# Routing filler, GpSimd subtractions tied to comparisons, and three 512-token tiles in a fused attention and two-MoE kernel

## The chip, the cores and the metric

The program runs on one core of one Trainium2 chip. The time is the device time of the program in microseconds, and each number for a kernel is the median of several runs. One further execution of the kernel was taken by the hardware profiler; all rows of the trace come from that one.

## The reference

```python
# attention: 4 batches, 8 heads, 576 positions, head size 64, causal window of 64
scores = q @ k.T / sqrt(64); softmax over the window; x = attn @ v     # 2304 tokens x 512
# dense layer
h = x @ w_in                                # 512 -> 2048
g = where(h > 0, h, exp(min(h, 0)) - 1)
x = g @ w_out                               # 2048 -> 512
# routed layer: 8 experts, 288 tokens each
logits = x @ w_gate
order = argsort(-logits.flatten())          # best token-expert pairs first
for idx in order:                           # greedy: a token takes the expert unless it is full
    tok, e = idx // 8, idx % 8
    if assigned[tok] >= 0 or counts[e] >= 288: continue
    assigned[tok] = e; counts[e] += 1
for e in range(8):
    out[mask_e] = relu(x[mask_e] @ w1[e]) @ w2[e]    # 512 -> 1024 -> 512
```

The assignment is a sequential greedy choice over 18432 pairs, so the logits must be very exact. The kernel therefore holds most operands as a pair of half-precision numbers, a high and a low part, and multiplies three of the four combinations.

## The kernel before

**Stages.** The tokens form 18 chunks of 128. Attention works chunk by chunk and writes its output, transposed, into tiles of tokens (`TILES`, line 360: five of 256 and two of 512). `layer1` (line 371) multiplies a tile by `w_in`, and ScalarE, GpSimd and VectorE make the activation and its two parts. `layer2` (line 447) multiplies by `w_out`, 48 matmuls of 512 columns for a chunk, and then leaves the chunk in three steps: ScalarE copies the sums out of PSUM, ScalarE rounds them to a high part, GpSimd subtracts to get the low part (line 469). A DMA writes both to `x2d` in DRAM (line 470). The last chunk alone uses VectorE for the low part (line 465). `gate` (line 412) computes the logits of a tile straight from the layer-1 result, with the matrix G2 that `prep_g2` (line 181) makes out of transposing DMAs into the one buffer `wt`; `x2_logits` does it for the first six chunks from `x2d`.

**Order.** `weave` (line 18) takes from several generators in proportion to declared totals, so the program order before line 950 is: `layer2` of tiles 0, 1, 2 and `layer1` of 3 and 4 between the attention chunks, then `layer1` of tiles 5 and 6. The framework's planner orders each engine's queue by priority and by its own estimate of times. From line 960 TensorE keeps the program order exactly (`pinned`).

**Routing** (line 546) needs all logits. It runs 7 phases; each finds a threshold in 5 digit steps and then does some bookkeeping. A digit step is a ring between two engines: VectorE makes the digit `D` (L612) and compares it with 32 values (L618); TensorE counts with 6 small matmuls (L621); VectorE reads the counts from PSUM (L625); 3 matmuls (L629); VectorE reads again (L631); 1 matmul (L635, or L638 in the last step). After the steps come L642 to L661, the matmuls L665 and L667, and L670 to L691, which give the value `M` for the next phase. In the phases from the fourth on, GpSimd does a part of that bookkeeping (L650 to L676 where `P_` stands, and L695 to L698 in all but the last). In the sixth phase GpSimd also makes two index tables (L701, L703). After the seventh phase VectorE builds the assignment (L706 to L716), TensorE sums it (L720, L721), VectorE makes positions and one-hot tables (L725 to L744), 18 matmuls (L748) turn them into row numbers, and L750 writes `idx`.

**Filler.** The small matmuls leave TensorE idle, so `fill` (line 950) lays the 576 matmuls of `layer2` for the last 12 chunks (1536 tokens) between them: each `yield W[n]` in the routing takes W[n] of them. The list `W` (line 948) gives 16 before and 8 inside the last gate, 33 before the phases, 69 in each phase (2 + 5 x 9 + 5 + 6 + 11), 4 and 3 at the two yields around L720, 6 and 4 around L748, and the 19 that remain follow when the routing is done. `dummies` (line 542) are matmuls whose results nobody reads, 8 at DM1 after L721 and 8 at DM2 after L748.

**Experts.** Each expert's weights come as four raw quarters of 1 MB into three buffers (`load_quarter`), and `split_expert` (line 773) turns each into high and low parts in 16 steps. During the filler experts 0 and 1 are split aside: ScalarE scales and rounds (L784, L785), GpSimd subtracts (L787), one step to every 17 filler matmuls. The other six are split by ScalarE and VectorE (L789, L790), two experts ahead of their use. `gather` (line 796) fetches the rows of an expert by `idx` from `x2d`; the first must wait for `idx` and for the last write to `x2d`.

Of the kernel before, what the change touches and what calls it, by code (L numbers as in the profile page):

```python
# [13 lines left out]
OP = mybir.AluOpType  # L14
# [25 lines left out]
def attention_moe_moe2_kernel(ctx: ExitStack, tc: tile.TileContext, q, k, v, w_in, w_out, w_gate, w1, w2, out):  # L40
# [316 lines left out]
    a2_ctx = ExitStack()  # L357

    NF32 = 2
    TILES = [256, 256, 256, 256, 256, 512, 512]  # L360
    T0 = [sum(TILES[:t]) for t in range(len(TILES))]


# [4 lines left out]
    def tile_n(t):  # L368
        return TILES[t]

# [73 lines left out]
            yield 300  # L444


    def layer2(t, chunks=None):
        fg = 1024 // tile_n(t)
        for i in range(tile_n(t) // 128) if chunks is None else chunks:
            c = T0[t] // 128 + i  # L450
            px = bank("mm", 3)
            m = 0
            for f in range(NF):
                g = GT[t][f // fg]
                for a, b in ((0, 0), (0, 1), (1, 0)):
                    pe(nc.tensor.matmul(px, g[:, f % fg, a, 128 * i:128 * i + 128], wo[f // 2][:, b, f % 2, :],  # L456
                                        start=m == 0, stop=m == 3 * NF - 1))
                    m += 1
                    yield 216
            xs = work.tile([128, 2, DM], F16, name="xs")  # L460
            x32 = work.tile([128, DM], F32, name="r", bufs=3)

            if c == NCH - 1:
                nc.scalar.activation(xs[:, 0], px, AF.Copy, scale=2.0 ** -11)
                nc.vector.scalar_tensor_tensor(xs[:, 1], px, 2.0 ** -11, xs[:, 0], op0=OP.mult, op1=OP.subtract)
            else:
                nc.scalar.activation(x32, px, AF.Copy, scale=2.0 ** -11)  # L467
                nc.scalar.activation(xs[:, 0], x32, AF.Copy)
                nc.gpsimd.tensor_tensor(xs[:, 1], x32, xs[:, 0], op=OP.subtract)
            nc.sync.dma_start(x2d[c * 128:(c + 1) * 128, :], xs.rearrange("p a d -> p (a d)"))  # L470

# [61 lines left out]
    def mid(ap, n):  # L535
        return ap[:, None, :].to_broadcast([ap.shape[0], n, ap.shape[1]])

    DM1 = 8
    DM2 = 8


# [4 lines left out]
    def routing():  # L546
# [50 lines left out]
        for ph in range(E - 1):  # L597
# [3 lines left out]
            for s in range(NS):  # L601
                ge = tl("ge", [128, NCH // 3, K, 3], BF, 2)
                if s == 0:
                    D, kk = M, r["k32"]
                else:

                    Mc = M
                    if s < NS - 1:
                        Mc = tl("Mc", [128, NCH], I32, 2)
                        V.tensor_scalar(Mc, M, -(K ** (NS - 1 - s)), None, op0=OP.bitwise_and)  # L610
                    D, kk = tl("D", [128, NCH], BF), r["k1" if s < NS - 1 else "k0"]
                    V.tensor_scalar(D, Mc, lo[:, 0:1], float(K) ** (s + 1 - NS), op0=OP.subtract, op1=OP.mult)  # L612
                pc = bank("sc", 2)
                for g0, g1 in ((0, SPL), (SPL, NCH // 3)):
                    if g0 == g1:
                        continue
                    d = D.rearrange("p (g i) -> p g i", i=3)[:, g0:g1, None, :].to_broadcast([128, g1 - g0, K, 3])
                    V.tensor_tensor(ge[:, g0:g1], d, kk[:, None].to_broadcast([128, g1 - g0, K, 3]), op=OP.is_ge)  # L618
                    yield W[3 if g0 == 0 else 4]
                    for g in range(g0, g1):  # L620
                        pe(T.matmul(pc[:3 * K, :3 * E], ge[:, g].rearrange("p k i -> p (k i)"),  # L621
                                    C[:, 3 * g:3 * g + 3].rearrange("p i e -> p (i e)"), start=g == 0,
                                    stop=g == NCH // 3 - 1))
                co = tl("co", [3 * K, 3 * E], F16)
                V.tensor_copy(co, pc[:3 * K, :3 * E])  # L625
                yield W[14]
                pk = bank("sc", 2)
                for i in range(3):
                    pe(T.matmul(pk[:K, :E], r["third"][:, i], co[:, i * E:(i + 1) * E], start=i == 0, stop=i == 2))  # L629
                full = tl("full", [K, E + 1], BF)  # L630
                V.tensor_scalar(full[:, :E], pk[:K, :E], float(CAP), 0.0, op0=OP.is_ge, op1=OP.max,  # L631
                                accum_out=full[:, E:])
                yield W[5]
                if s < NS - 1:
                    pe(T.matmul(lo[:, 0:1], r["wt"][:, s], full[:, E:], start=s == 0, stop=True, skip_group_check=True))  # L635
                else:
                    hi = bank("tp", 2)
                    pe(T.matmul(hi[:, :E + 1], r["ones"][:K], full, start=True, stop=True))  # L638
# [81 lines left out]
        pe(T.matmul(pr[:, :E], r["one"], r["ebase"][0:1], start=True, stop=False))  # L720
        pe(T.matmul(pr[:, :E], r["tri"], rk[:, :, NCH - 1], start=False, stop=True))  # L721
        yield W[16]
        dummies(DM1)
        t = tl("ts", [128, E, NCH])
        V.tensor_tensor(t, rk, bc(pr[:, :E], NCH), op=OP.add)  # L725
        V.tensor_tensor(t, t, AT_, op=OP.mult)
# [46 lines left out]
    def split_expert(e, aside=False):  # L773
        W1[e], W2[e] = [], []
        for i in range(4):
            st = RAW[e, i].rearrange("p (g n) -> p g n", n=512)
            for g in range(4):
# [4 lines left out]
                if aside:  # L782
                    with tc.issue_after(last["act"]):
                        nc.scalar.activation(st[:, g], st[:, g], AF.Copy, scale=64.0)  # L784
                        nc.scalar.activation(t[:, 0, c], st[:, g], AF.Copy)  # L785
                    with tc.issue_after(last["pool"]):
                        nc.gpsimd.tensor_tensor(t[:, 1, c], st[:, g], t[:, 0, c], op=OP.subtract)  # L787
                else:
                    dv(nc.scalar.activation(t[:, 0, c], st[:, g], AF.Copy, scale=64.0))  # L789
                    dv(nc.vector.scalar_tensor_tensor(t[:, 1, c], st[:, g], 64.0, t[:, 0, c], op0=OP.mult,  # L790
                                                      op1=OP.subtract))
                if g == 3:
                    load_quarter()
                yield 500

# [132 lines left out]
    def attend(a, b):  # L928
        return attention(range(a, b)), (b - a) * AT
# [4 lines left out]
          (chain(split_win(), *(prep_wout(j) for j in range(4))), 24), attend(A0, A1))  # L934
    w64_ctx.close()
    a2.append(a2_ctx.enter_context(tc.tile_pool(name="a2", bufs=2)))
    weave((layer2(0), UT), attend(A1, A1 + 2))
    weave((layer2(1), UT), attend(A1 + 2, A1 + 5))
    weave((chain(layer1(3), layer2(2)), 2 * UT), attend(A1 + 5, A1 + 9), (prep_g2(range(NF)), NF * 8 * 75))
    weave((chain(layer1(4), gate(3), gate(4)), UT * 1.25), attend(A1 + 9, NCH + 1), (x2_logits(range(6)), 18 * 100))  # L940
    a2_ctx.close()
    att_ctx.close()
    late = ExitStack()
    slabB = late.enter_context(tc.tile_pool(name="slabB", bufs=10))
    rpool = late.enter_context(tc.tile_pool(name="rpool", bufs=2))
    routing_consts(rpool)
    weave((chain(layer1(5, [slabB] * 8), gate(5), layer1(6, [slabB] * 2 + [slabA] * 6)), UT * 3))
    W = [1, 4, 2, 5, 0, 2, 5, 6, 11, 4, 16, 2, 6, 4, 2, 28, 3]

    def fill():  # L950
        for _ in range(3):
            load_quarter()
        p = chain(split_expert(0, True), split_expert(1, True))
        for i, _ in enumerate(chain(*(layer2(t) for t in range(3, 7)))):
            if i % 17 == 16 and i < 24 * 17:
                next(p, None)
            yield
        weave((p, 1))
# [2 lines left out]
    xs = fill()  # L961
    for _ in range(W[10]):
        next(xs, None)
    for _ in gate(6):
        for _ in range(W[11]):
            next(xs, None)
    rt_gen = routing()
# [5 lines left out]
            next(xs, None)  # L973
    for _ in xs:
        pass
    pinned.clear()
    late.close()
    moe = ctx.enter_context(tc.tile_pool(name="moe", bufs=2))
# [2 lines left out]
    for e in range(E):  # L981
# [3 lines left out]
        ss = [(expert(e, xe_first() if e == 0 else None, tail if e == E - 1 else None), 24000.0)]  # L985
        if e + 1 < E:
            gather(e + 1)
        sp = split_expert(e + 2) if e < E - 2 else iter(())
        ss.append((chain(take(sp, 8 if e < E - 2 else 0), xe_t(e + 1) if e < E - 1 else iter(()), sp), 9400.0))
        if e > 0:  # L990
            ss.append((o_rows(e - 1), 2000.0))
        weave(*ss)
# [31 lines left out]
```

## Time and profile before

| what | value |
|---|---|
| median of 3 runs | 821.84 us (820.53 to 821.99) |
| profiled execution | 817.73 us, its span 816.0 us |
| TensorE busy | 762.2 us (93%) |
| VectorE, ScalarE, GpSimd busy | 444.8, 368.6, 214.7 us |
| mean granted TensorE clock | 0.973 of full speed |

The span runs from the first to the last instruction. [...]

### The profile page before, as it was taken

Reading aid. Unit: us, or ns where it says so; the run is one execution under the profiler, and the core shown is the slowest. Engines: PE = TensorE matmul, PEld = TensorE weight load, DVE = VectorE, ACT = ScalarE, POOL = GpSimd, SP = SyncE. Lnnn points to the kernel's source line nnn. Section 1 sums busy time; section 2 is a strip of 40 time slices with the busy share of each in tenths; the row PEclk is TensorE's granted clock in tenths of the full one; section 3 lists DMA queues with packets and bytes.
Section 4 is the critical chain, followed back from the end, with each engine's and each line's share of the span. In section 5 each row is a group of like instructions: output and inputs, shape, how many; then the busy total and the mean of one; then the engine's idle time right before and its main releaser. Section 6 shows DMA issues by size and latency. Waiting matters only on the chain. (4 is left out here: it accounts for less than half of the span.)

```text
span 816.0 us, 16645 instructions
## 1 busy us (share of the span) xinstructions
PE 762.2 (93%) x6746; PEld 508.6 (62%) x6746; DVE 444.8 (55%) x1091; ACT 368.6 (45%) x895; POOL 214.7 (26%) x323
## 2 busy tenths in 40 slices
PE   7888899899998999999998999998759999999996
PEld 4666688645786587545453444443338888888886
DVE  4886599821465346554555565565806555546110
ACT  3556775714654446444466230100205665556222
POOL 3000002121031032644576342324532212221002
PEclk9999999799999999999999999999869999999999
DMA  9998134506365344001023230000329789997001
GB/s 241 300 266 213 25 99 169 104 24 133 86 139 104 77 92 104 2 1 52 1 91 129 78 117 27 14 27 14 103 88 209 238 245 273 198 248 196 20 21 50
DMA packets 122509, 94.23 MB, mean 115 GB/s; under 512 B 99200, under 2 KB 99200, under 8 KB 122432
## 3 DMA queue, kind: packets, MB, share of 16 engines
q1 hardware_dynamic: 119360, 83.72, 39.4%
q0 software_dynamic: 3072, 9.44, 4.3%
q8 instruction: 53, 0.87, 0.4%
q14 instruction: 24, 0.20, 0.1%
HBM read 69.22 MB, written 9.44 MB: 96 GB/s over the span
## 5 line engine op out<-in xcount | busy, mean ns | idle before, releaser
L456 PE MATMUL ps_mm<-slab,g 128*128 128x512 f16 x864 | 214.3, 382 | 0.0
L401 PE MATMUL ps_mm<-xt,slab 128*128 128x256 f16 (+1 forms) x960 | 154.7, 317 | 0.0
L401 PEld LDWEIGHTS <-slab 128*128 128x128 f16 x960 | 91.1, 98 | 49.0 <-issue 0.8
L456 PEld LDWEIGHTS <-g 128*128 128x128 f16 x864 | 74.6, 99 | 75.2 <-issue 7.2
L855 PE MATMUL ps_mm<-xet,slab 128*128 128x288 f16 (+1 forms) x840 | 101.6, 279 | 0.0
L406 POOL TENSOR_SCALAR r<-r 128x512 f32<-128x512 f32 x56 | 41.5, 742 | 198.2 <-ACT r L405 197.7
L889 PEld LDWEIGHTS <-slab 128*128 128x128 f16 x960 | 78.6, 98 | 16.2
L855 PEld LDWEIGHTS <-slab 128*128 128x128 f16 x840 | 77.7, 100 | 17.5
L790 DVE SCALAR_TENSOR_TENSOR slab<-raw,slab 128x512 f16<-128x512 f32 x96 | 62.5, 688 | 16.9 <-ACT slab L789 14.9
L861 DVE SCALAR_TENSOR_TENSOR h<-ps_mm,h 128x288 f16<-128x288 f32 x64 | 29.3, 457 | 76.7 <-ACT h L860 75.5
L889 PE MATMUL ps_sc<-h,slab 128*128 128x288 f16 (+1 forms) x480 | 70.1, 262 | 0.0
L889 PE MATMUL ps_tp<-h,slab 128*128 128x288 f16 (+1 forms) x480 | 69.8, 262 | 0.0
L404 ACT ACTIVATE r<-ps_mm 128x512 f32<-128x512 f32 x56 | 33.7, 605 | 74.8 <-PE ps_mm L401 51.6
L287 ACT ACTIVATE sm<-ps_sc,mx 128x128 f32<-128x128 f32 x144 | 50.8, 380 | 26.3 <-DVE mx L285 26.0
L389 PE MATMUL ps_mm<-xt,slab 128*128 128x256 f32 x256 | 61.1, 394 | 0.8 <-DVE slab L107 0.8
L409 DVE TENSOR_TENSOR g<-r,g 128x512 f16<-128x512 f32 x56 | 39.1, 704 | 38.2 <-POOL g L408 38.1
L467 ACT ACTIVATE r<-ps_mm 128x512 f32<-128x512 f32 x17 | 10.2, 600 | 103.8 <-PE ps_mm L456 103.7
L789 ACT ACTIVATE slab<-raw 128x512 f16<-128x512 f32 x96 | 55.3, 621 | 0.0
L389 PEld LDWEIGHTS ps_mm<-xt,slab 128*128 128x128 f32 x256 | 49.0, 196 | 9.3 <-issue 1.1
L407 DVE TENSOR_TENSOR r<-ps_mm,r 128x512 f32<-128x512 f32 x56 | 38.5, 690 | 29.3 <-POOL r L406 29.3
L830 POOL DMA_INDIRECT out_dram<-orow,idx x24 | 22.2, 924 | 114.4 <-ACT orow L844 112.7
L408 POOL TENSOR_SCALAR g<-r 128x512 f16<-128x512 f32 x56 | 35.7, 641 | 52.6 <-DVE r L407 32.8
(208 smaller groups left out, 1143.0 us busy)
## 6 DMA issues: line engine op xcount, KB each, us to landing
raw<-in_moe_w_dram SPq DMA_DIRECT2D x32, 1024.0 KB, 6.1
slab<-in_moe_w_in_dram SPq DMA_DIRECT2D x16, 512.0 KB, 7.4
st<-in_moe_w_out_dram SPq DMA_DIRECT2D x16, 512.0 KB, 3.9
x2d<-xs SPq DMA_DIRECT2D x18, 256.0 KB, 3.1
vp<-vn SPq DMA_DIRECT2D x35, 128.0 KB, 3.8
qn<-in_q_dram SPq DMA_DIRECT2D x16, 256.0 KB, 4.6
kn<-in_k_dram SPq DMA_DIRECT2D x16, 256.0 KB, 3.6
vn<-in_v_dram SPq DMA_DIRECT2D x16, 256.0 KB, 3.1
```

Of the source, the lines that this page charges most:

```text
L287: nc.scalar.activation(P[c, blk][:, i], SC[blk][:, i], AF.Exp, bias=mx[:, blk, i:i + 1], accum_out=rs[:, blk, i:i + 1])
L389: nc.tensor.matmul(ph[:, i], wi32[d, (f + i) // 8].bitcast(F32)[:, c], XT[t][:, d, :n], start=d == 0, stop=d == ND - 1)
L401: nc.tensor.matmul(ph[:, i], wi[d, (f + i) // 8][:, a, (f + i) % 8 * 128:((f + i) % 8 + 1) * 128], XT[t][:, b, d, :n], start=m == 0, stop= ...
L406: nc.gpsimd.tensor_scalar(r, r, -1.0, A_H, op0=OP.add, op1=OP.mult)
L407: nc.vector.tensor_tensor(r, ph, r, op=OP.max)
L408: last["pool"] = nc.gpsimd.tensor_scalar(hi, r, 1.0, 1.0, op0=OP.mult, op1=OP.mult).ins
L409: nc.vector.tensor_tensor(lo, r, hi, op=OP.subtract)
L456: pe(nc.tensor.matmul(px, g[:, f % fg, a, 128 * i:128 * i + 128], wo[f // 2][:, b, f % 2, :], start=m == 0, stop=m == 3 * NF - 1))
L789: dv(nc.scalar.activation(t[:, 0, c], st[:, g], AF.Copy, scale=64.0))
L790: dv(nc.vector.scalar_tensor_tensor(t[:, 1, c], st[:, g], 64.0, t[:, 0, c], op0=OP.mult, op1=OP.subtract))
L855: nc.tensor.matmul(ph[:, r], W1[e][d][:, a, f * 128:(f + 1) * 128], XET[e][:, b, d, r], start=m == 0, stop=m == 3 * ND - 1)
L889: nc.tensor.matmul(po[:, :n], w[:, a, f % 2, d * 128:(d + 1) * 128], H2[e][:, b, f, r], start=m == 0, stop=m == 3 * NF2 - 1)
```

## The change

The token tiles become three of 256 and three of 512, and the stages before the routing are dealt out anew. During the filler, the GpSimd subtractions, those of `layer2` and those of the aside split, are put on a list `later`. In each digit step, after the first comparison is issued, one is taken off the list with a dependency on that comparison; what must follow it (the DMA to `x2d`, the load of the next quarter) is issued with it. Only expert 0 is split aside, one step to every 24 filler matmuls; expert e + 1 is split within expert e. The dummies at DM1 go. `W` takes 73 filler matmuls in each phase (3 + 5 x 9 + 6 + 6 + 13), 4 and 4 around L720, and none around L748: 576 in all by then.

```diff
-    TILES = [256, 256, 256, 256, 256, 512, 512]
+    TILES = [256, 256, 256, 512, 512, 512]
...
+    later = []
+    def low_parts(behind=None):
+        lo, v, hi, then = later.pop(0)
+        ins = nc.gpsimd.tensor_tensor(lo, v, hi, op=OP.subtract)
+        if behind is not None:
+            tc.add_manual_dep(ins.ins, behind.ins.name, mybir.DependencyInfo(
+                mybir.DependencyClass.Sync, mybir.DependencyReason.SCHED_ONLY), reason="beside PSUM reads")
+        if then is not None:
+            then()
...                                                            # layer2
-                nc.gpsimd.tensor_tensor(xs[:, 1], x32, xs[:, 0], op=OP.subtract)
-            nc.sync.dma_start(x2d[c * 128:(c + 1) * 128, :], xs.rearrange("p a d -> p (a d)"))
+                later.append((xs[:, 1], x32, xs[:, 0], lambda c=c, xs=xs: out(c, xs)))
+                if not pinned:
+                    low_parts()
+                continue
+            out(c, xs)
...                                                            # routing, digit step
-                    V.tensor_tensor(ge[:, g0:g1], d, kk[:, None].to_broadcast([128, g1 - g0, K, 3]), op=OP.is_ge)
+                    cmp = V.tensor_tensor(ge[:, g0:g1], d, kk[:, None].to_broadcast([128, g1 - g0, K, 3]), op=OP.is_ge)
+                    if later and g0 == 0:
+                        low_parts(cmp)
...
-        dummies(DM1)
...                                                            # split_expert
-                    with tc.issue_after(last["pool"]):
-                        nc.gpsimd.tensor_tensor(t[:, 1, c], st[:, g], t[:, 0, c], op=OP.subtract)
+                    later.append((t[:, 1, c], st[:, g], t[:, 0, c], load_quarter if g == 3 else None))
...
-                if g == 3:
+                if g == 3 and not aside:
                     load_quarter()
...                                                            # order of the stages
-    weave((layer2(0), UT), attend(A1, A1 + 2))
-    weave((layer2(1), UT), attend(A1 + 2, A1 + 5))
-    weave((chain(layer1(3), layer2(2)), 2 * UT), attend(A1 + 5, A1 + 9), (prep_g2(range(NF)), NF * 8 * 75))
-    weave((chain(layer1(4), gate(3), gate(4)), UT * 1.25), attend(A1 + 9, NCH + 1), (x2_logits(range(6)), 18 * 100))
+    weave((layer2(0), UT), attend(A1, A1 + 3))
+    weave((layer2(1), UT), attend(A1 + 3, A1 + 6))
+    weave((layer2(2), UT), attend(A1 + 6, A1 + 9), (prep_g2(range(NF)), NF * 8 * 75))
+    weave((chain(after(9), layer1(3), gate(3)), UT * 2.25), attend(A1 + 9, NCH + 1), (x2_logits(range(6)), 18 * 100))
...
-    weave((chain(layer1(5, [slabB] * 8), gate(5), layer1(6, [slabB] * 2 + [slabA] * 6)), UT * 3))
-    W = [1, 4, 2, 5, 0, 2, 5, 6, 11, 4, 16, 2, 6, 4, 2, 28, 3]
+    weave((chain(layer1(4, [slabB] * 8), gate(4), layer1(5, [slabB] * 2 + [slabA] * 6)), UT * 4))
+    W = [1, 4, 3, 5, 0, 2, 6, 6, 13, 4, 16, 2, 0, 0, 2, 28, 4]
...                                                            # fill
-        p = chain(split_expert(0, True), split_expert(1, True))
-        for i, _ in enumerate(chain(*(layer2(t) for t in range(3, 7)))):
-            if i % 17 == 16 and i < 24 * 17:
+        p = split_expert(0, True)
+        for i, _ in enumerate(chain(*(layer2(t) for t in range(3, 6)))):
+            if i % 24 == 23:
                 next(p, None)
...                                                            # after the routing; expert loop
+    while later:
+        low_parts()
...
-        sp = split_expert(e + 2) if e < E - 2 else iter(())
-        ss.append((chain(take(sp, 8 if e < E - 2 else 0), xe_t(e + 1) if e < E - 1 else iter(()), sp), 9400.0))
+        sp = split_expert(e + 1) if e < E - 1 else iter(())
+        ss.append((chain(take(sp, 8 if e < E - 1 else 0), xe_t(e + 1) if e < E - 1 else iter(()), sp), 9400.0))
```

## Rows read from the trace of the kernel before

**Rows 1.** Busy time of the engine, share of the span, instructions.

```profile
PE 762.2 (93%) x6746; PEld 508.6 (62%) x6746; DVE 444.8 (55%) x1091; ACT 368.6 (45%) x895; POOL 214.7 (26%) x323
```

**Rows 2.** Busy time of each engine by stretch, then granted clock, DMA share, GB/s.

```profile
440.00:460.00 20.00, 17.47 (x112) 7.65 (x111) 12.81 (x45) 8.16 (x15) 8.72 (x11) 1.00 0.34 119
580.00:600.00 20.00, 16.73 (x67) 8.44 (x66) 8.77 (x14) 2.79 (x5) 5.27 (x4) 0.83 0.31 106
600.00:620.00 20.00, 13.44 (x179) 12.12 (x180) 5.93 (x12) 5.32 (x12) 9.86 (x10) 0.74 0.64 130
```

**Rows 3.** Timeline of TensorE, routing: start, length, line, tiles, count, [idle before].

```profile
432.12 0.40 PE L621 MATMUL ps_sc<-C,ge 128*96 128x24 bf16 x6
...
534.56 0.40 PE L621 MATMUL ps_sc<-C,ge 128*96 128x24 bf16 x6
...
553.50 0.40 PE L621 MATMUL ps_sc<-C,ge 128*96 128x24 bf16 x6
...
572.37 0.18 PE L667 MATMUL ps_sc<-rk,tri 128*128 128x8 bf16 x1
```

**Rows 4.** Timeline of VectorE, first phase: two digit steps, then a disturbed one.

```profile
435.12 0.55 DVE L618 TENSOR_TENSOR ge<-D,k 128x576 bf16<-128x576 bf16 x1
...
437.44 0.24 DVE L612 TENSOR_SCALAR D<-Mc,ps_pv 128x18 bf16<-128x18 int32 x1 [0.48 <-PE ps_pv L635]
...
438.86 0.18 DVE L625 CAST co<-ps_sc 96x24 f16<-96x24 f32 x1 [0.59 <-PE ps_sc L621]
...
440.54 1.46 DVE L618 TENSOR_TENSOR ge<-D,k 128x576 bf16<-128x576 bf16 x1
```

**Rows 5.** Timeline of GpSimd, the same stretch, and its index tables later.

```profile
438.19 4.78 POOL L787 TENSOR_TENSOR slab<-raw,slab 128x512 f16<-128x512 f32 x4 [1.54 <-ACT slab L785]
...
553.27 3.70 POOL L701 IOTA i<- 128x432 f16 x2
```

**Rows 6.** Timeline of VectorE, end of the seventh phase and assignment.

```profile
570.16 0.23 DVE L648 TENSOR_TENSOR U<-C,cl 128x144 bf16<-128x144 bf16 x1
...
577.31 1.18 DVE L711 TENSOR_TENSOR A<-A,done 128x144 bf16<-128x144 bf16 x1
...
582.51 1.34 DVE L737 TENSOR_TENSOR oh<-gr,i 128x432 f16<-128x432 f16 x1
...
585.04 3.38 DVE L744 TENSOR_TENSOR oB<-sa,i 128x864 f16<-128x864 f16 x2
```

**Rows 7.** Timeline of GpSimd, from the assignment to the first gather.

```profile
574.86 4.64 POOL L787 TENSOR_TENSOR slab<-raw,slab 128x512 f16<-128x512 f32 x4
...
602.79 1.17 POOL L800 DMA_INDIRECT xe<-x2d,idx  x1 [15.07 <-issue]
```

**Rows 8.** Timeline of TensorE, from the sum of the assignment to the first expert.

```profile
580.67 0.17 PE L721 MATMUL ps_sc<-rk,tri 128*128 128x8 bf16 x1 [4.56 <-DVE rk L716]
...
589.35 1.62 PE L748 MATMUL ps_sc<-oA,oB 128*96 128x24 f16 x9
...
594.02 4.26 PE L456 MATMUL ps_mm<-slab,g 128*128 128x512 f16 x19
...
606.24 0.80 PE L812 MATMUL ps_tp<-ident,xe 96*128 96x96 f16 x8 [7.95 <-DMA xe<-x2d,idx]
```

**Rows 9.** Timeline of TensorE, layer 1 in both tile sizes, and a transpose's wait.

```profile
239.26 2.56 PE L401 MATMUL ps_mm<-xt,slab 128*128 128x256 f16 x22
...
248.03 0.18 PE L190 MATMUL ps_tp<-wgs,wt 128*128 128x16 f16 x1 [2.35 <-DMA wt<-slab]
...
399.82 14.19 PE L401 MATMUL ps_mm<-xt,slab 128*128 128x512 f16 x65
```

**Rows 10.** Timeline of the queue of SyncE, the transposes of that stretch.

```profile
242.03 12.39 SPq L186 DMA_TRANSPOSE wt<-slab  x2
```

**Rows 11.** Timeline of VectorE and TensorE, experts 0 and 1.

```profile
625.26 4.91 DVE L790 SCALAR_TENSOR_TENSOR slab<-raw,slab 128x512 f16<-128x512 f32 x8
...
633.41 4.57 PE L855 MATMUL ps_mm<-xet,slab 128*128 128x288 f16 x36
```

More of the change, by code (lines that the diff above doesn't have):

```diff
@@ L444, in x2_logits, with out @@
             yield 300
+    later = []
[7 more added lines that the diff above has]
+            then()
     def layer2(t, chunks=None):
+        def out(c, xs):
+            nc.sync.dma_start(x2d[c * 128:(c + 1) * 128, :], xs.rearrange("p a d -> p (a d)"))
         fg = 1024 // tile_n(t)
@@ L536, in mid @@
         return ap[:, None, :].to_broadcast([ap.shape[0], n, ap.shape[1]])
-    DM1 = 8
     DM2 = 8
@@ L963, in attention_moe_moe2_kernel @@
         next(xs, None)
-    for _ in gate(6):
+    for _ in gate(5):
         for _ in range(W[11]):
```

## The prediction

> **What bounds the kernel now.** I read the page's busy line first: TensorE is busy 93% of the span [rows 1], so there is little to win except where it stands idle or runs at the lower clock. [...] The chain of waits, read backwards, passes through the experts as one TensorE stream and leaves TensorE at the first gather. So three timelines follow.
>
> In the phases, the first small matmuls (L621) begin at 432.12 in phase one, 534.56 in phase six, 553.50 in phase seven [rows 3]. Phase six took 18.94 us and has no wait of TensorE in it; the six phases before 553.50 took 121.38, so 121.38 - 6 x 18.94 = 7.74 us are lost. The reader sees the cause in VectorE's rows: a comparison takes 0.55 us, but 1.46 us while four subtractions of GpSimd run (4.78 us, 1.2 each), whereas the read of PSUM in the same stretch keeps its 0.18 [rows 4, 5].
>
> At the end, a VectorE step on 128x144 takes 0.23 us undisturbed; the five such steps of the assignment take about 1.2 (1.18 in the row), beside four more subtractions, from the late steps of expert 1 [rows 6, 7]. TensorE waits 4.56 us for them [rows 8]. After L721 at 580.67, tables (L737 to L744), L748, sixteen dummies and 32 filler matmuls follow, and the last of these end at 598.28; the last chunk then goes through ScalarE, VectorE and a DMA to the gather at 602.79, and TensorE starts expert 0 at 606.24 after 7.95 us idle [rows 7, 8].
>
> **The change part by part.** A filler matmul takes (4.26 - 0.17) / 19 = 0.215 us [rows 8].
>
> *Subtractions behind comparisons.* A comparison ends at 435.67, and the next instruction that reads SBUF for the ring, the digit, starts at 437.44 [rows 4]: a window of 1.77 us for a subtraction of 1.2. Between lie only the two PSUM reads, which GpSimd did not slow. Of the 27 subtractions (11 chunks, 16 split steps), 4.5 fall to a phase with 5 slots, so the list stays short. The phase loss of 7.74 us goes. What the wait holds up on GpSimd is its share of the bookkeeping (needed a phase-end later) and on SyncE the writes to x2d and the quarter loads, which nothing in the phases waits for; I cost them at 0. The bounds for collisions that stay: 0, if all fit, to 27 x (1.46 - 0.55) = 24.6 us, if each holds a comparison. I take 1.5, near the lower end, because phase six has a subtraction and GpSimd's bookkeeping in it and loses nothing. The index tables in phase seven (3.70 us [rows 5]) are not tied to anything; that phase's length from L621 to L667, 18.87 us, stays.
>
> [...]
>
> *73 instead of 69 filler matmuls in a phase.* 28 more come before L721. 26 of them come before the last L667: 26 x 0.215 = 5.6 us later, since TensorE is the bound in an undisturbed phase. L667 of phase seven moves from 572.37 [rows 3] by -7.74 + 5.6 to 570.2.
>
> *From L667 to L721.* Before: 8.30 us. TensorE now has 13 + 4 filler matmuls there, 3.7 us. VectorE's chain without GpSimd: five steps lose 1.18 - 0.23 = 0.95 us each [rows 6], 4.75 in all, so it ends 8.30 - 4.75 = 3.55 us after L667. TensorE is the later: 3.8 us, L721 at 574.0, 6.7 us earlier than before.
>
> *From L721 to the gather.* Before: 22.12 us. The four last filler matmuls end 1.0 us after L721, so the dummies of DM1 and the 28 filler matmuls behind them leave this path; what covered their time is that they were the path. VectorE reaches L737 at 1.84 us, as before. At the rate of the comparison, 576 elements in 0.55 us [rows 4], the two of 432 take 0.41 each and the two of 864 take 0.83 each, not 1.34 and 1.69 [rows 6]: tables done at 4.3. Then nine L748 in 1.6 [rows 8] and idx: 6.3. The other condition is the last write to x2d: before, 4.51 us passed from the last filler matmul to the gather. If VectorE takes the last chunk's low part at once, that gives 5.5 and idx decides (6.3); if it comes behind the tables, 4.3 + 3.8 = 8.1. I take 8.1, because the routing has priority over it. The gather then starts at 574.0 + 8.1 = 582.1 instead of 602.79: 20.7 us earlier.
>
> *Start of expert 0.* The gap before it shrinks from 7.95 to about 3 us. The clock stood at 0.74 in that stretch [rows 2]: 26% below full is 10.4 us at half, a part of which may return. Between 0 and 3 us; I take 1.
>
> *Splits.* Expert 1 is split within expert 0, where expert 2 was split: the same 16 steps. They ended at 630.2 and expert 1 starts at 633.4 [rows 11], so its first weights are there in time, and the second half is needed only in its second layer. Expert 6 gets a split that it did not have: VectorE has 16 steps of 0.61 (4.91 / 8) more in an expert of 26 us, (816.0 - 633.4) / 7; TensorE stays the bound, 0. Without that cover it would be 10 us at most.
>
> *Three tiles of 512.* 384 matmuls at (2.56 - 0.17) / 22 = 0.1086 become 192 at (14.19 - 0.17) / 65 = 0.2157 [rows 9]: 0.3 us less. The stages before the routing are dealt out differently; prep_g2 now lies beside one layer-2 tile instead of two tiles. A transpose issued at 242.03 was awaited until 248.03 and cost 2.35 us [rows 9, 10]. Bounds: -4 (that wait and its low clock vanish) to 7 x 2.35 = 16.5 (each later one waits so). I take 0: that wait was the longest of eight transposes, and the planner moves other work ahead.
>
> *Sum:* -20.7 + 1.5 - 1 - 0.3 = -20.5 us. For an execution like the profiled one, span 816.0 and 817.73 in all, that is 797.2. The median of the runs lies 4.1 above that execution, so 821.84 - 20.5 = 801.
>
> **The rivals.**
>
> 1. The collisions move instead of going. A subtraction that starts more than 0.57 us after its comparison (1.77 - 1.2), because ScalarE or the bookkeeping was late, holds the digit or the next comparison. For: batches of ScalarE work on the raw quarters, and 27 subtractions in 35 slots. Against: the queue is short. If the phases lose as much as before, 7.7 instead of 1.5, the time is 807.
>
> 2. The same mechanism in nearly every step: 24.6 us instead of 1.5 gives 824, slower than before. The place is the step from L618 to L612; the point from which it decides is 23 of the 27 held for 0.91 us, (20.5 + 1.5 - 1) / 0.91. Against it speaks that the wait ends with the comparison itself.
>
> 3. The transposes of prep_g2 become the bound of their stage: seven need 6 us each between issue and use, 42 us, and layer 2 of one tile, 96 x 0.215 = 20.6 us, with three attention chunks may not cover that. At 16.5 us the time is 818; if each wait costs its length again in lost clock, 834.
>
> 4. The list does not shorten the end: VectorE's slow tables are slow for themselves, and the gather stays 22 us behind L721 less the 28 filler matmuls (6.0). Then -6.7 - 6.0 + 1.5 - 0.3: 810. The 4.64 us of subtractions beside the slow steps [rows 7] speak against it.
>
> 5. VectorE takes the last chunk at once and the early waits shrink: -1.8 - 4 more: 795.
>
> **How the numbers follow.** Forecast 0.60, rival 1 0.15, rival 2 0.04, rival 3 0.06, rival 4 0.05, rival 5 0.10. The forecast alone reaches from 797 (idx decides, no collision) to 806 (three more microseconds of collisions, two of early waits). The range 792 to 814 takes in rivals 1, 4 and 5. About 0.2%, 1.6 us, is what a measurement of this kernel can tell from no change. Rivals 2 and 3 hold the rest: 0.07 slower (rival 2 and half of rival 3), 0.03 within (the other half); faster by more 0.90.
>
> **What would show it.** Right: comparisons of 0.55 to 0.6 us throughout; L621 to L621 of 19.8 us in the phases; no wait of TensorE at L721; L744 below 1 us each; L721 to gather 6 to 9 us; first gather near 582. Wrong: D or L618 of over 1 us beside a subtraction, waits for wt above 5 us in all, a wait of expert 1 for its weights, or a routing that starts later than before.

## The result, and the profile after

The changed kernel takes 799.99 us (median of 4 runs, 798.05 to 801.85) against 821.91 us of the kernel before beside it: a ratio of 0.9729, 95% interval 0.9694 to 0.9764. Timed once more (e11) it took 800.26 us, ratio 0.9756 [0.9724, 0.9788]. The forecast was 801. The profiled execution took 798.05 us, its span 796.3 us, where the prediction's sum for such an execution gave 797.2 and 795.5.

Busy times, after (they answer [rows 1]): TensorE does 200 instructions fewer and its share rises from 93 to 95%.

```profile
PE 752.9 (95%) x6546; PEld 487.3 (61%) x6546; DVE 437.9 (55%) x1107; ACT 361.4 (45%) x879; POOL 197.4 (25%) x307
```

By stretch, after (they answer [rows 2], and two stretches more). At 440 us TensorE is now busy all of the time. At the end 17.02 and 17.82 are left (16.73 and 13.44 in the last two stretches before). A new weak place, at 340 us, was busy 20.00 of 20 at a granted clock of 1.00 before.

```profile
340.00:360.00 20.00, 14.98 (x85) 6.91 (x86) 11.92 (x15) 8.14 (x14) 10.98 (x21) 0.78 0.01 2
440.00:460.00 20.00, 20.00 (x131) 8.89 (x130) 10.45 (x50) 4.89 (x9) 7.68 (x10) 1.00 0.24 79
560.00:580.00 20.00, 17.02 (x105) 8.35 (x103) 13.65 (x48) 1.82 (x3) 3.11 (x7) 0.94 0.07 27
580.00:600.00 20.00, 17.82 (x195) 14.38 (x195) 5.95 (x12) 5.00 (x11) 10.42 (x10) 0.80 0.47 120
```

Timeline of TensorE, after (it answers [rows 3, 8]; L641 was L621, L687 was L667, L741 was L721, L767 was L748, L830 was L812). Phases one and two start 19.52 us apart, six and seven 19.58; one longer wait is left, in phase seven; the sum L741 waits for nothing; the gather's transposes start at 586.47 instead of 606.24. Rows of matmuls that follow each other overlap: L687 begins at 570.34 and lasts 0.18 us, the next row begins at 570.37; so the 17 of L472 there take (3.83 - 0.18) / 17 = 0.215 us each.

```profile
436.18 0.40 PE L641 MATMUL ps_sc<-C,ge 128*96 128x24 bf16 x6
455.70 0.40 PE L641 MATMUL ps_sc<-C,ge 128*96 128x24 bf16 x6
...
533.91 0.40 PE L641 MATMUL ps_sc<-C,ge 128*96 128x24 bf16 x6
...
553.49 0.40 PE L641 MATMUL ps_sc<-C,ge 128*96 128x24 bf16 x6
...
557.98 0.44 PE L641 MATMUL ps_sc<-C,ge 128*96 128x24 bf16 x6 [1.66 <-DVE ge L636]
...
570.34 0.18 PE L687 MATMUL ps_sc<-rk,tri 128*128 128x8 bf16 x1
570.37 3.83 PE L472 MATMUL ps_mm<-slab,g 128*128 128x512 f16 x17
...
574.45 0.18 PE L741 MATMUL ps_sc<-rk,tri 128*128 128x8 bf16 x1
...
578.49 3.42 PE L767 MATMUL ps_sc<-oA,oB 128*96 128x24 f16 x18 [2.98 <-DVE oB L763]
...
586.47 0.50 PE L830 MATMUL ps_tp<-ident,xe 96*128 96x96 f16 x8 [1.50 <-DMA xe<-x2d,idx]
```

VectorE, after (it answers [rows 4, 6]). The comparison L636 keeps 0.56 us, the assignment's step L731 its 0.23 (1.18 before), the tables L756 and L763 take 0.38 and 0.73 each (1.34 and 1.69 before). L481, the last chunk's low part, stands ahead of the tables. The two rows at 555 and 556 us are the collisions that are left.

```profile
440.83 0.56 DVE L636 TENSOR_TENSOR ge<-D,k 128x576 bf16<-128x576 bf16 x1
...
443.22 0.24 DVE L630 TENSOR_SCALAR D<-Mc,ps_pv 128x18 bf16<-128x18 int32 x1 [0.48 <-PE ps_pv L655]
...
555.17 1.17 DVE L630 TENSOR_SCALAR D<-Mc,ps_pv 128x18 bf16<-128x18 int32 x1 [0.48 <-PE ps_pv L655]
556.38 1.08 DVE L628 TENSOR_SCALAR Mc<-M 128x18 int32<-128x18 int32 x1
...
572.82 0.23 DVE L731 TENSOR_TENSOR A<-A,done 128x144 bf16<-128x144 bf16 x1
...
576.23 0.69 DVE L481 SCALAR_TENSOR_TENSOR xs<-ps_mm,xs 128x512 f16<-128x512 f32 x1
...
576.92 0.38 DVE L756 TENSOR_TENSOR oh<-gr,i 128x432 f16<-128x432 f16 x1
...
577.63 1.46 DVE L763 TENSOR_TENSOR oB<-sa,i 128x864 f16<-128x864 f16 x2
581.94 0.18 DVE L769 TENSOR_SCALAR idx<-ps_sc 96x24 int32<-96x24 f32 x1 [2.85 <-PE ps_sc L767]
```

GpSimd, after (it answers [rows 5, 7]). A subtraction (L452) starts 0.15 us after the comparison that ends at 441.39 and is over at 442.69, before the digit at 443.22. The constants at 335.81 had waited 12.56 us; the index table of 552.61 ends at 556.31; the gather waits for `idx`.

```profile
335.81 1.83 POOL L510 IOTA k<- 128x96 f32 x3 [12.56 <-PE ps_pv L307]
...
441.54 1.15 POOL L452 TENSOR_TENSOR xs<-r,xs 128x512 f16<-128x512 f32 x1 [1.46 <-DVE ge L636]
...
552.61 3.70 POOL L721 IOTA i<- 128x432 f16 x2
556.27 1.16 POOL L452 TENSOR_TENSOR xs<-r,xs 128x512 f16<-128x512 f32 x1
...
583.08 1.17 POOL L818 DMA_INDIRECT xe<-x2d,idx  x1 [12.71 <-DVE idx L769]
```

To compare kernels, I divide each profiled execution at the starts of five rows: the first matmul of layer 2, the first digit matmul, the last prefix matmul (L687), the sum (L741), the first gather; and take the time from the expert's first transposes to the end. What lies ahead of the first layer-2 matmul takes 162 to 169 us from one execution to the next, of either kernel, so the early stages are measured from there.

| us | median | layer 2 to digit | to L687 | to sum | to gather | expert to end |
|---|---|---|---|---|---|---|
| before | 821.91 | 270.1 | 140.3 | 8.3 | 22.1 | 209.8 |
| after | 799.99 | 273.3 | 134.1 | 4.1 | 8.6 | 209.8 |
| e1 no wait | 804.66 | 273.5 | 140.2 | 4.1 | 8.6 | 209.8 |
| e2 wait for the sum | 812.78 | 273.3 | 147.7 | 4.1 | 8.6 | 209.7 |
| e3 old tiles | 795.79 | 270.5 | 135.7 | 4.1 | 8.6 | 208.2 |
| e4 constants later | 800.04 | 272.1 | 134.2 | 4.1 | 8.6 | 208.1 |
| e5 before, one expert | 809.95 | 270.7 | 137.5 | 4.6 | 17.9 | 209.9 |
| e6 after, two experts | 808.00 | 273.3 | 139.3 | 7.1 | 8.6 | 210.9 |
| e7 before, new filler | 814.63 | 270.2 | 147.6 | 7.0 | 9.3 | 210.0 |
| e8 old tiles, dummies | 797.25 | 270.0 | 134.2 | 4.1 | 8.7 | 210.0 |
| e9 after, old filler | 809.94 | 273.0 | 133.4 | 4.6 | 19.5 | 209.8 |
| e10 old tiles again | 798.04 | 269.8 | 134.2 | 4.1 | 8.7 | 209.8 |
| e11 after again | 800.26 | 273.5 | 134.2 | 4.1 | 8.6 | 209.8 |

So 13.5 us came from the end (sum to gather), 4.2 from the stretch ahead of the sum, 6.2 from the phases, and some 3 went back before the routing.

### The profile page after: what moved, and what is told of

Its sections match the earlier page's. It is cut to its first block, busy times and chain, and to the rows that moved or that the text cites. A ratio compares the mean times of both kernels' runs of the same rounds, so it can differ in the third digit from the quotient of the medians.

```text
span 796.3 us, 16214 instructions
## 1 busy us (share of the span) xinstructions
PE 752.9 (95%) x6546; PEld 487.3 (61%) x6546; DVE 437.9 (55%) x1107; ACT 361.4 (45%) x879; POOL 197.4 (25%) x307
## 4 chain that ended last, share of the span: by engine, by line
PE 77%; DVE 7%; ACT 5%; DMA 4%; issue 2%; SPq 2%; POOL 2%; POOLq 0%; DVEq 0%; ACTq 0%
PE ps_mm L472 24%; PE ps_mm L401 15%; PE ps_mm L873 12%; PE ps_sc L907 6%; PE ps_tp L907 6%; DMA slab<-in_moe_w_in_dram 2%; PE ps_mm L389 2%; PE ps_pv L307 2%; ACT sm L287 2%; PE ps_tp L298 2%; DMA st<-in_moe_w_out_dram 1%; ACT slab L111 1%; PE ps_pv L860 1%; PE ps_sc L641 1%; DVE b L107 1%
## 5 line engine op out<-in xcount | busy, mean ns | idle before, releaser
L472 PE MATMUL ps_mm<-slab,g 128*128 128x512 f16 x864 | 211.8, 380 | 0.0
L401 PE MATMUL ps_mm<-xt,slab 128*128 128x512 f16 (+1 forms) x768 | 152.1, 355 | 2.1 <-DVE r L407 2.1
L472 PEld LDWEIGHTS <-g 128*128 128x128 f16 x864 | 74.0, 98 | 69.8 <-issue 1.5
L401 PEld LDWEIGHTS <-slab 128*128 128x128 f16 x768 | 72.8, 98 | 67.5 <-issue 5.0
L907 PEld LDWEIGHTS <-slab 128*128 128x128 f16 x960 | 78.6, 98 | 16.2
L873 PEld LDWEIGHTS <-slab 128*128 128x128 f16 x840 | 77.7, 100 | 17.6
L808 DVE SCALAR_TENSOR_TENSOR slab<-raw,slab 128x512 f16<-128x512 f32 x112 | 72.9, 688 | 20.2 <-ACT slab L807 17.8
L807 ACT ACTIVATE slab<-raw 128x512 f16<-128x512 f32 x112 | 64.5, 621 | 0.0
```

What stands on the lines that cost most here:

```text
L401: nc.tensor.matmul(ph[:, i], wi[d, (f + i) // 8][:, a, (f + i) % 8 * 128:((f + i) % 8 + 1) * 128], XT[t][:, b, d, :n], start=m == 0, stop= ...
L873: nc.tensor.matmul(ph[:, r], W1[e][d][:, a, f * 128:(f + 1) * 128], XET[e][:, b, d, r], start=m == 0, stop=m == 3 * ND - 1)
L907: nc.tensor.matmul(po[:, :n], w[:, a, f % 2, d * 128:(d + 1) * 128], H2[e][:, b, f, r], start=m == 0, stop=m == 3 * NF2 - 1)
```

## The experiments

**e1: the list without its wait.** A subtraction is still issued in the digit step, but starts when its operands are there.

```diff
-                        low_parts(cmp)
+                        low_parts()
```

> The changed kernel, but the subtractions in the digit steps are issued at the same places without waiting for the comparison. Theory (the wait is what keeps GpSimd off VectorE's comparisons): subtractions start when ScalarE has rounded, at any point of a step; comparisons or digits of 0.9 to 1.5 us return, the six phases take 121 us again instead of 117.3, and the time is 804 to 808. Rival (fewer subtractions, spread over the steps, suffice; the wait does nothing): comparisons stay at 0.56, six phases within 0.5 us of 117.3, time within 1.6 us of the changed kernel.

Measured: 804.66 us (802.54 to 806.46), 0.979 [0.9765, 0.9814]. GpSimd in e1, then VectorE, then TensorE: eight subtractions run through, the comparison beside them takes 1.50 us, and TensorE waits for it. The phases are back at 140.2 us: the first six take 121.2, as expected, and phase seven 19.0 instead of 16.85. The end is as short as in the changed kernel. The wait itself is worth some 5 us by the ratios and 6.1 by the phases; the rest of the gain does not hang on it.

```profile
462.98 9.91 POOL L452 TENSOR_TENSOR slab<-raw,slab 128x512 f16<-128x512 f32 x8
```

```profile
463.05 1.50 DVE L636 TENSOR_TENSOR ge<-D,k 128x576 bf16<-128x576 bf16 x1
```

```profile
464.60 0.44 PE L641 MATMUL ps_sc<-C,ge 128*96 128x24 bf16 x6 [0.86 <-DVE ge L636]
```

**e2: the same wait at the wrong place.** The subtraction waits for the last PSUM read of the step (L649 here) instead of the comparison.

```diff
-                    if later and g0 == 0:
-                        low_parts(cmp)
...
-                V.tensor_scalar(full[:, :E], ...
+                seen = V.tensor_scalar(full[:, :E], ...
...
+                if later:
+                    low_parts(seen)
```

> The changed kernel, but each subtraction waits for the second read of PSUM (L651) and not for the comparison. [...] Rival (the ring has slack enough, or only long collisions count): under 5 us more.

Measured: 812.78 us (811.16 to 813.49), 0.989 [0.9868, 0.9912]. GpSimd, then VectorE: the subtraction runs from 442.81 to 443.97, the digit from 443.14 to 443.99 (0.85 us instead of 0.24). It comes back in step after step, 13.6 us over the phases; the time is a little below the 814 to 818 of my estimate. This is rival 2's mechanism: in the changed kernel a subtraction of 1.15 us that starts 0.15 us after the comparison is over before the digit, here one of 1.16 us that starts 1.45 us after it is not.

```profile
442.81 1.16 POOL L452 TENSOR_TENSOR slab<-raw,slab 128x512 f16<-128x512 f32 x1 [2.15 <-DVE full L649]
```

```profile
443.14 0.85 DVE L630 TENSOR_SCALAR D<-Mc,ps_pv 128x18 bf16<-128x18 int32 x1 [0.48 <-PE ps_pv L655]
```

**e3 and e10: the old tiles and stage order, the rest as changed**, the second time beside e11.

```diff
-    TILES = [256, 256, 256, 512, 512, 512]
+    TILES = [256, 256, 256, 256, 256, 512, 512]
...                                  # and the weave lines of the kernel before
```

> The changed kernel with the tiles (five of 256, two of 512) and the order of the stages of the kernel before. Theory (the new tiles and order cost 4 us ahead of the routing, where the first L641 came at 436.2 instead of 432.1): the first L641 near 432, the rest unchanged, time 4 us below the changed kernel, 796. Rival (512-column tiles are the gain they look, and the 4 us come from another part): within 1.6 us or slower.

> The kernel with the old token tiles and stage order, everything else as changed, a second time and beside the changed kernel. Theory: the new tiles and order cost 3 to 4 us before the routing, so it is 3 to 5 us below the changed kernel: 795 to 797. Rival: the first time was low by chance, both agree within 1.6 us, near 799.

> The changed kernel again, as the yardstick on this chip. Theory and rival alike: 798 to 802, ratio to the kernel before 0.970 to 0.976.

Measured: e3 795.79 us (792.78 to 797.59), 0.968 [0.9647, 0.9712]; e10 798.04 us (793.88 to 799.12), 0.9711 [0.9678, 0.9744], against 800.26 us (799.51 to 804.59) of e11 on the same chip. From layer 2 to the first digit they need 270.5 and 269.8 us, e11 273.5. So this part of the change costs some 3 us; by the medians 2.2 (e10 and e11) to 4.2 (e3 and the first runs of the changed kernel). The 3 to 5 us that were expected between e10 and e11 did not come in full, but every run of e10 lies below every run of e11. The 1.6 us by which e3 and e4 are shorter in the experts are not in e10, so they aren't put down to the edit. e10 pays the wait for `wt` of [rows 9] again, 2.38 us, and TensorE then is busy 20.00 us of 20 from 340 us on.

```profile
253.34 0.18 PE L190 MATMUL ps_tp<-wgs,wt 128*128 128x16 f16 x1 [2.38 <-DMA wt<-slab]
```

The changed kernel has no such wait, but these, TensorE at 340 us, in the gate and layer 1 of the tile that comes next; with two of 0.33 us they make 6.05 us, and the granted clock is 0.78 from 340 to 360 us, 0.50 from 340 to 348.

```profile
340.39 0.23 PE L419 MATMUL ps_tp<-G,g 128*128 128x16 f16 x2 [1.41 <-POOL g L408]
342.83 0.19 PE L420 MATMUL ps_tp<-G,g 128*128 128x8 f16 x1 [2.22 <-DVE g L409]
...
346.01 4.18 PE L401 MATMUL ps_mm<-xt,slab 128*128 128x512 f16 x12 [1.76 <-DVE r L407]
```

**e4: why those waits are there.** My theory was that the routing's constants, which stood 12.56 us in GpSimd's queue until attention's last matmul had been done with their memory, held up layer 1 behind them. They are issued after the last layer-1 tiles here.

```diff
-    routing_consts(rpool)
     weave((chain(layer1(4, [slabB] * 8), gate(4), layer1(5, [slabB] * 2 + [slabA] * 6)), UT * 4))
+    routing_consts(rpool)
```

> The changed kernel, but the routing's constants are issued after the last layer-1 stage instead of before it, so that GpSimd's last three roundings of the fourth tile (L408) stand ahead of the constants in its queue. Theory (these roundings wait behind constants whose buffers come free only when attention ends, and TensorE waits 6.0 us for them and then runs at half clock): most of the waits of TensorE between 338 and 346 us go, time 5 to 9 us below the changed kernel, 791 to 795. Rival (gate 3 stands too close behind its layer 1 and waits anyway): under 2 us.

Measured: 800.04 us (797.23 to 800.78), 0.9731 [0.9704, 0.9759]: nothing gained in the time, the theory fell. GpSimd in e4, the first row: now layer 1's own step waits as long for the same matmul. These three rows of it are the first of the next tile, where I had expected the last of the fourth: in the changed kernel the fourth tile's sixteen were over at 311.67. By the kernel's order the step writes into `slabB`, which takes the memory that attention's buffers leave. The constants' place counts for little: TensorE's waits there are 3.54 us instead of 6.05, and the stretch from layer 2 to the digit is 272.1 us, against 273.0 to 273.5 in the other six with these tiles.

The wait for that buffer is not new. The second row is the kernel before: the same step waits for the same matmul, but only 2.11 us (e3 and e10 too). Attention's last matmul lets go at the same place in both, 172.5 and 172.9 us behind the first layer-2 matmul; GpSimd is done with what lies ahead of it at 332.41 before and at 323.25 after. So what the new order changed is that layer 1 gets there about 10 us too early. Other memory for `slabB`, or a later start of this layer 1, was not tried.

```profile
341.20 2.28 POOL L408 TENSOR_SCALAR g<-r 128x512 f16<-128x512 f32 x3 [12.58 <-PE ps_pv L307]
```

```profile
334.51 1.78 POOL L408 TENSOR_SCALAR g<-r 128x512 f16<-128x512 f32 x3 [2.11 <-PE ps_pv L307]
```

**e5: the kernel before with only one expert split aside.**

```diff
-        p = chain(split_expert(0, True), split_expert(1, True))
+        p = split_expert(0, True)
...
-        sp = split_expert(e + 2) if e < E - 2 else iter(())
+        sp = split_expert(e + 1) if e < E - 1 else iter(())
...                                  # and its share of the weave
```

> The kernel before with one part of the change: only expert 0 is split aside, expert e + 1 within expert e. 27 subtractions of GpSimd in the routing instead of 43, none late, and no wait for comparisons. Theory (the slow end of the seventh phase comes from expert 1's late subtractions, the loss in the phases from collisions at any time): L667 to L721 falls from 8.3 to about 4 us, the stretch from the first L621 to the last L667 loses about half of its excess (140.3 to 137 us), L721 to gather stays at 20 to 22 us since filler matmuls and dummies are its path; 7 to 10 us faster than before, 811 to 814. Rival (the number of subtractions matters little): 819 or more.

Measured: 809.95 us (806.38 to 815.42), 0.9865 [0.9779, 0.995]. By the medians about half of the gain (the interval is 4 to 18 us) comes from taking 16 subtractions away: 2.8 us in the phases, 3.7 ahead of the sum, and 4.2 behind it, where 2 at most were expected. GpSimd in e5 shows what is left: the gather waits for the last write to `x2d`.

```profile
597.90 1.17 POOL L800 DMA_INDIRECT xe<-x2d,idx  x1 [19.98 <-DMA x2d<-xs]
```

**e6: the changed kernel with two experts aside**, one step to every 17 filler matmuls, as before.

```diff
-        p = split_expert(0, True)
+        p = chain(split_expert(0, True), split_expert(1, True))
-            if i % 24 == 23:
+            if i % 17 == 16:
...                                  # and expert e + 2 split within expert e
```

> The changed kernel with experts 0 and 1 split aside, one step to 17 filler matmuls, and expert e + 2 within expert e, as before. 43 subtractions for 35 slots: 8 or more are left on the list when the phases end, and they are issued before the first gather; the last chunks' low parts stand behind split steps in the list. Theory (the list overflows, so the gather is late): no collisions in the phases (134 us from the first L641 to the last L687), but L741 to gather grows from 8.6 to 13 to 20 us; time 5 to 12 us above the changed kernel, 805 to 812. Rival (what is left over hides beside the tables): within 1.6 us, 800.

Measured: 808.00 us (806.7 to 809.82), 0.9853 [0.9786, 0.9919]. The time was as expected, the place was not: the gather is no later behind the sum (8.6 us). GpSimd, then TensorE in phase seven: the steps run out while the list is still full, and the rest runs through beside the bookkeeping, which TensorE then waits for.

```profile
564.89 2.37 POOL L452 TENSOR_TENSOR xs<-r,xs 128x512 f16<-128x512 f32 x2 [4.67 <-DVE ge L636]
...
576.65 2.42 POOL L452 TENSOR_TENSOR slab<-raw,slab 128x512 f16<-128x512 f32 x2
```

```profile
573.67 0.23 PE L685 MATMUL ps_sc<-mc,ones 128*128 128x48 bf16 x3 [1.72 <-POOL mc L670]
582.10 0.18 PE L741 MATMUL ps_sc<-rk,tri 128*128 128x8 bf16 x1 [2.89 <-DVE rk L736]
```

**e7: the kernel before with the new filler alone.**

```diff
-        dummies(DM1)
...
-    W = [1, 4, 2, 5, 0, 2, 5, 6, 11, 4, 16, 2, 6, 4, 2, 28, 3]
+    W = [1, 4, 3, 5, 0, 2, 6, 6, 13, 4, 16, 2, 0, 0, 2, 28, 4]
```

> The kernel before with one part of the change: the filler list that ends with the phases, and no dummies at DM1. Both experts are split aside, GpSimd doesn't wait. Theory (28 filler matmuls cost 6 us where TensorE is the bound, and the end is then held by VectorE's tables, still slowed by GpSimd): first L621 to last L667 140 + 5.6 us, L667 to L721 about 8, L721 to gather 12 to 14 instead of 22; 2 to 6 us faster, 815 to 819. Rival (the filler alone is the gain): over 10 us faster, below 811.

Measured: 814.63 us (810.39 to 817.22), 0.991 [0.9873, 0.9946]. The gather comes 9.3 us behind the sum instead of 22.1, but the phases take 7.3 us more (5.6 were expected). The subtractions of two experts now have to fit into them: in e1, where the same filler meets those of one expert, the phases take 140.2 us instead of 147.6 (e1 has the new tiles and places of issue too). TensorE in e7:

```profile
441.50 0.44 PE L621 MATMUL ps_sc<-C,ge 128*96 128x24 bf16 x6 [1.48 <-DVE ge L618]
```

**e9: the changed kernel with the old filler.**

```diff
+    DM1 = 8
...
+        dummies(DM1)
...
-    W = [1, 4, 3, 5, 0, 2, 6, 6, 13, 4, 16, 2, 0, 0, 2, 28, 4]
+    W = [1, 4, 2, 5, 0, 2, 5, 6, 11, 4, 16, 2, 6, 4, 2, 28, 3]
```

> The changed kernel with the filler dealt out as before: 69 filler matmuls in a phase instead of 73, 6 and 4 around the matmuls of the row numbers, 19 behind the routing, and the 8 dummies after the sum of the assignment. Theory: the phases shrink by what 28 filler matmuls took, 19.5 - 18.94 = 0.56 us for each of the first six and the rest behind them, 4 to 5.5 us up to the last L667; but the last filler matmul then comes 28 x 0.215 = 6.0 us and the dummies' 1.0 us later after the sum, so that the last write to x2d decides again: sum to gather 8.6 + 7 = 15.6 us. Together +1.5 to +3 us: 801.5 to 803. Rival: once GpSimd is out of the way the writes of the last chunk are quick enough and the rows still wait for idx alone; then the gather stays 8.6 to 10 us behind the sum and the time falls to 795 to 796.

Measured: 809.94 us (803.79 to 814.44), 0.9858 [0.9818, 0.9898], further up than the 801.5 to 803 of the theory, whose direction held. The phases are only 0.8 us shorter than in the changed kernel: each of the first six takes 18.9 us, but phase seven falls into a wait of 2.11 us again. The gather comes 19.5 us behind the sum. GpSimd in e9: nothing but the last write to `x2d` holds it.

```profile
599.46 1.17 POOL L820 DMA_INDIRECT xe<-x2d,idx  x1 [21.57 <-DMA x2d<-xs]
```

**e8: e3 with 13 dummies ahead of L767**, to test whether its 18 matmuls take 3.42 us because TensorE had stood idle for 2.98 us before them.

```diff
+    DM1 = 13
...
+        dummies(DM1)
...                                  # and the tiles and weave lines of e3
```

> The changed kernel with the old tiles and order of the stages, as in e3, and 13 dummies after the four last filler matmuls, where the change took 8 away. Theory (after L741 TensorE stands idle for 3.0 us and L767 then runs at half clock, 0.18 us each): the dummies end before the first table is ready, the 18 L767 take 1.6 to 2.0 us in all instead of 3.3, and L741 to gather falls from 8.6 to 7.2; time 1.4 us below e3, 794. Rival (dummies delay L767 or the clock isn't what makes it slow): L741 to gather at 8.6 or more.

Measured: 797.25 us (795.79 to 798.77), 0.9717 [0.9651, 0.9784]: no gain, the theory fell. TensorE in e8: the dummies fill the gap and the 18 still take 3.42 us. The granted clock is no reason either: it was 1.00 in their first 1.7 us in e8 and 0.66 then, 0.50 all along in the changed kernel. The second fence is the weight load of the same matmuls and of a filler matmul in the changed kernel (mean ns of one): 276 against 97 ns. The weight loads are busy 3.30 of the 3.30 us from 578.50 on. So by these rows the matmuls go as fast as their weights come; why these come slowly was not tested.

```profile
573.73 2.97 PE L563 MATMUL ps_mm<-slab 128*128 128x512 f16 x13
576.92 3.42 PE L769 MATMUL ps_sc<-oA,oB 128*96 128x24 f16 x18 [0.22 <-DVE oB L765]
```

```profile
L767 PEld LDWEIGHTS <-oB 128*96 128x96 f16 x18 | 3.3, 276 | 3.5 <-DVE oB L763 3.5
...
L472 PEld LDWEIGHTS <-g 128*128 128x128 f16 x4 | 0.3, 97 | 0.2
```

## Why the prediction was right

The time and the main mechanism were right; several terms were off by 1 to 3.5 us each way and cancel: the span came out at 796.3 where the sum gave 795.5. That it is so near is luck.

- *Subtractions behind comparisons.* Right, and better than costed. The loss of 7.74 us in the first six phases went in full, and the 1.5 us of collisions taken as left did not come: six phases take 117.3 us. The bound of 24.6 us was not idle: e2 pays 13.6 of it by waiting for a read that ends 1.3 us after the comparison. In e2 the digit of 443.14 takes 0.85 us instead of 0.24 and ends 0.02 us after the subtraction, while PSUM reads keep their 0.18 us beside subtractions (before, 438.86). Why the one is held and the other is not, no run shows.
- *73 filler matmuls in a phase.* Four cost 19.55 - 18.94 = 0.6 us, not 0.86; six phases make 1.5 us of gain. Why is open. TensorE is busy without a gap from 436 to 553 us; the view of the line L641 has 10.7 us of waits in 29 of the 35 digit steps, but 9.0 of them, in 28 steps, are its weight loads', beside filler matmuls that go on.
- *Phase seven.* Taken at 18.87 us and one of the added filler matmuls, 0.22, measured 16.85. This term was mis-sized by 2.24 us. The index table still holds the digit (1.17 us, 1.82 before), and TensorE's wait is 1.66 us, 2.12 before: 0.5 us. Behind the 2.12 us the granted clock was 0.66 in the next 4 us, and the next two steps took 3.91 and 3.03 us; behind the 1.66 us it stayed at 1.00 and they took 2.70 and 2.67. So 1.6 us of it is clock that did not fall. The last 0.2 is the filler matmul that was added, which cost nothing: the last step takes 4.32 us in both. The part of the clock is luck: e3 has the same wait of 1.66 us at the same matmul, the clock was 0.73 behind it, and its phase seven took 1.5 us more. The 4 us behind the wait by stretch, of before, of after and of e3:

```profile
558.40:562.40 4.00, 3.96 (x20) 1.58 (x21) 1.15 (x5) 0.00 (x0) 0.97 (x1) 0.66 0.19 70
```

```profile
558.00:562.00 4.00, 4.00 (x32) 1.80 (x32) 1.49 (x8) 0.00 (x0) 0.67 (x1) 1.00 0.17 66
```

```profile
557.20:561.20 4.00, 4.00 (x26) 1.94 (x27) 1.14 (x5) 0.00 (x0) 0.67 (x1) 0.73 0.17 66
```

  The wait in e3:

```profile
557.18 0.44 PE L641 MATMUL ps_sc<-C,ge 128*96 128x24 bf16 x6 [1.66 <-DVE ge L636]
```

- *L687 to the sum.* Forecast 3.8 us by TensorE's 17 filler matmuls, measured 4.1, no wait: right.
- *Sum to gather.* Forecast 8.1, measured 8.6, but the number is nearer than its reason. I let the write to `x2d` decide; L481 came ahead of the tables, as in rival 5, and `idx` decided, which I had at 6.3. The tables were done 4.64 us behind the sum (4.3 forecast), the matmuls 2.82 later (1.6), and the gather started 1.17 behind them (0.4). So the step that failed most is the "nine L748 in 1.6": the first nine start at 578.49, but they are not over when the second table is, at 579.09; all 18 take 3.42 us from the first table on. e8 shows that no idle time before them is to blame.
- *Start of expert 0.* Forecast 1 us, measured 0: gather to end is 213.2 us in both kernels (816.0 - 602.79 and 796.3 - 583.08), although the gap shrank from 7.95 to 1.50 us. The idle time that vanished was already counted as the earlier gather; and though the granted clock in the 20 us from the first transposes was 0.91 instead of 0.88, no time came back. The low clock that the forecast drew on is in the trace of before, 0.50 from 602 to 610 us and 1.00 from 612 to 620; that the shorter gap would give a part of it back was my estimate.
- *Splits.* Right: the experts take 209.8 us in both.
- *Tiles and stages.* Forecast -0.3, measured +3.2. The `wt` wait (2.35 us before, the granted clock 0.50 from 250 to 252 us behind it) did vanish, as its lower bound had it, and rival 3's transposes cost nothing; but the new order made GpSimd wait 12.56 us for attention's memory, where it had waited 2.11, and TensorE behind it; no bound of mine named that wait. e3 and e10 confirm the size; by e4 the constants are about 1 us of it. That the buffer is the rest is read from the rows, not tested.

Of the rivals, 2 is refuted by the rows of the changed kernel, 4 by the tables, which were slow for GpSimd's sake (1.69 to 0.73 us), and by e7: the filler's end alone brings the gather from 22.1 to 9.3 us. Of rival 1's collisions the changed kernel has one, the copy L628 of 1.08 us at 556.38; e1 shows them without the wait. Of rival 5 the half about the last chunk came true, the half about the early waits did not.

The parts don't add up one by one. Each against the runs of before beside it, the filler alone gives 6.2 us (e7), one expert less alone 10.8 (e5), all but the wait 16.2 (e1), the whole 21.9. Taken out of the changed kernel, the filler is worth more, 9.7 (e9 against e11 on the same chip). The filler's end and the split compete for the phases; only when GpSimd has little to do there, and does it at the right time, is the end to be had without paying for it there. The best version measured keeps the old tiles: 795.79 and 798.04 us, against 799.99 and 800.26.

## What to carry to other kernels

When two engines get in each other's way, look in the waiting engine's ring for a step that the other does not lengthen (here the PSUM read, 0.18 us with a subtraction beside it and without), and tie the other engine's work to the instruction just before that step; tied 1.3 us later it cost more than no tie at all (812.78 against 804.66 us). Independent work that fills a wait belongs into stretches whose end depends on another engine, and none of it behind the point where its own result is awaited. When a stage order is dealt out anew, follow not only data but memory: which new buffer takes the place of which old one, who still reads that, and how early the new order gets there: the same wait was 2.11 us in one order and 12.56 in the other.

## What was not expected of the hardware

- A GpSimd instruction that only writes (the index table, 552.61 to 556.31) held VectorE's digit, which has one input from SBUF and one from PSUM, until its end: 555.17 + 1.17 = 556.34, where a digit takes 0.24 us otherwise. The row after it, the copy L628, was held likewise by a subtraction: 556.38 + 1.08 = 557.46, and the subtraction ends at 557.43.
- The same wait of TensorE at the same matmul of the loop, 1.65 to 1.66 us, was followed over 4 us by a granted clock of 1.00 in five executions (after, e4, e8, e10, e11) and of 0.73 in one (e3). Behind 2.12 us (before) and 2.11 us (e9) it was 0.66 and 0.50. One profile without the fall does not show that the next has none.
- The 18 matmuls of 24 columns went as fast as their weights came: 3.42 us with weight loads of 276 ns, whether TensorE was idle (after) or busy (e8) before them, and at a granted clock of 0.50 (after) as at 1.00 and then 0.66 (e8). L641's weights, 128x96 too, load in 125 ns.
